# The low part of the attention output in the first four chunks: by a product with minus one and a copy, in place of a subtraction

## The chip, the cores and the metric

The kernel runs on one core of a Trainium2 chip. The time is the device time of one execution in microseconds; several executions are timed and the median is given. Of one more execution there is a profile, with the start and duration of every instruction on every engine. The engines are TensorE (PE in the profile; its weight loads have a row of their own, PEld), VectorE (DVE), ScalarE (ACT), GpSimd (POOL) and SyncE (SP, which here only issues transfers). PSUM is the memory into which TensorE writes, in eight banks of 128 x 512 words; SBUF holds everything else.

## What is computed

A recurrence over time (linear attention with a decay per channel and a bonus `u` for the current step), and behind it a block with a hidden layer, a convolution over three steps in time and a gate:

```python
for t in range(S):                                   # B=4, H=8, S=768, D=48
    kt, vt, rt, wt = (k[:, :, t], v[:, :, t], r[:, :, t], w[:, :, t])
    cur = np.einsum('bhd,bhe->bhde', u[None] * kt, vt)
    y[:, :, t] = np.einsum('bhd,bhde->bhe', rt, state + cur)
    state = wt[:, :, :, None] * state + np.einsum('bhd,bhe->bhde', kt, vt)
x = y.transpose(0, 2, 1, 3).reshape(B, S, 384)
h = np.maximum(x @ w_in, 0)                          # 384 -> 1024
conv_out = sum(conv_w[j] * shifted(h, j - 1) for j in range(3))
out = (h * sigmoid(conv_out)) @ w_out                # 1024 -> 384
```

The inputs are drawn as float32 for `r`, `k`, `v`, `w` and `u`; the three weights of the block come as float64.

## The kernel before, in words

**Chunks.** The recurrence is taken in chunks of 128 time steps, six to each of the four batches, 24 in all. `stage_a` (lines 527 to 605) loads `w`, `k`, `r` of a chunk, turns them with TensorE (L542), forms the running products of the decays with two scans on VectorE (L549, L556; between them L553 writes the reciprocal of a chunk's whole decay into the buffer `dA`, which L556 reads), scales keys and queries (L554, L560), and writes the diagonal of the bonus on GpSimd (L581, L583, L587). `stage_b` (lines 607 to 746) forms the products of keys and queries (L660), masks them on VectorE (L664), carries the state (L636, L639, L677, L681) and makes the output `y` of the chunk, turned, in a bank of PSUM.

**High and low parts.** The block's products take numbers of the type float32r. To keep the accuracy, every factor is split: a high part, which is the number cast to float32r, and a low part, the difference of the number and its high part. A product of two factors is then three products, high by high, high by low and low by high (`product_in`, L753, and `product_out`, L782). The tile `xT` holds the chunk outputs, turned, with high (index 0) and low (index 1) parts beside each other; `wi` and `wo` hold the weights, split in the same way (L456 casts, L457 subtracts), after they have been put together from the words of the float64 (L436 to L450).

**The first four chunks** (`n < EARLY`, with `EARLY = 4`) are made in another layout than the rest, so that the first block needs no transfer from SBUF to SBUF. Their `y` is made in rows of 128 by L690, L693, L700 and L705. ScalarE copies it as the high part into `xT` (L708); VectorE subtracts that from `y` for the low part (L709). The other twenty chunks do the same in L731 and L733.

**Blocks.** Eight blocks of 384 time steps follow their chunks. Each goes through eight slices of the hidden layer: three times three products (L753), relu, convolution and gate on ScalarE and VectorE (L765 to L772), the split (L774, L775); then the products with `wo` (L782), a copy (L812) and the transfer out (L813). The first block needs the chunks 0 to 3, since the convolution reaches one step beyond its 384.

**The order.** Nothing of this is issued as it is written. Each step is put into a plan with `op(engine, cost, function, reads, writes, ...)`, with a cost in microseconds from the table `LEN` and a rank (chunk n: 14 n; its second stage 7 later; a block 5 per slice later still). `Plan.issue` (lines 139 to 221) then runs a list scheduler: each engine takes, of the steps that are ready and for which a buffer is free, the one of lowest rank. Steps of TensorE count 1.4 times their cost in the first 60 us (`COLD`). The order thus found is the fixed order of each engine's queue. Buffers come from kinds with a number of places (`Kind`): eight PSUM banks shared by five kinds, two places for `dA` and so on; a place comes free when the last step that uses it is done. A changed cost, step or number of places can change the order of everything after it.

Ahead of the plan, the constants are made, among them the 128x128 identity `ident` on GpSimd.

Of the kernel before, what the change touches and what calls it, by code (L numbers as in the profile page):

```python
# [9 lines left out]
F32 = mybir.dt.float32  # L10
BF16 = mybir.dt.bfloat16
F32R = mybir.dt.float32r
# [3 lines left out]
ALU = mybir.AluOpType  # L16
# [19 lines left out]
    stt=0.54, gate=0.47, wts=0.47, wstt=0.47,  # L36
    fill=0.25, kh=0.42, guard=0.72, sbd=0.34, xhi=0.49, relu=0.5, mul=0.49, sig=0.43, cast=0.42, out=0.37, exp=0.52,
    z=0.98, diag=1.07, lo=0.97,
    gather=1.6, carried_rows=1.4, y_rows=1.5,
    load=0.55, issue=0.45, spread=0.64,  # L40
)
TAIL = dict(PE=0.22, DVE=0.11, ACT=0.13, POOL=0.07, SP=2.2)
# [66 lines left out]
class Plan:  # L109
# [6 lines left out]
    def op(self, eng, us, f, r=(), w=(), holds=(), moves=0.0, port=False, rank=None):  # L116
        i, deps = len(self.ops), set()
        us = LEN[us] if isinstance(us, str) else us
        for t in r:
            if t in self.last:  # L120
                deps.add(self.last[t])
            self.readers.setdefault(t, []).append(i)
        for t in w:
            if t in self.last:
                deps.add(self.last[t])
            deps.update(self.readers.get(t, ()))
            self.last[t], self.readers[t] = i, []
        deps.discard(i)
        bufs = []
        for t in (*r, *w, *holds):  # L130
            if isinstance(t, Buf) and t not in bufs:
                bufs.append(t)
                t.uses += 1
                if t.turn is None:
                    t.turn = t.kind.wanted
                    t.kind.wanted += 1
        self.ops.append((eng, us, f, deps, bufs, moves, port, (self.rank if rank is None else rank) + i * 1e-6))
# [159 lines left out]
def rwkv_conv_moe_kernel(  # L297
# [12 lines left out]
    nc = tc.nc  # L310
# [3 lines left out]
    P = 128  # L314
# [5 lines left out]
    KT = DM // P  # L320
    WID = KT * SL + 1
# [8 lines left out]
    fconst = fast.enter_context(tc.tile_pool(name="fconst", bufs=1))  # L330
# [8 lines left out]
    for _ in range(WARM):  # L339
# [8 lines left out]
    ident = const.tile([P, P], F32, name="ident")  # L348
# [5 lines left out]
                            fill=0.0, base=0, channel_multiplier=-1)  # L354
# [13 lines left out]
    guard_hi = fconst.tile([P, 1], F32, name="guard_hi")  # L368
    nc.vector.memset(guard_hi, -W_HI)
    flags = fconst.tile([P, N, 2], F32, name="flags")  # L370

    xT = const.tile([P, 2 * KT + 1, 2, SP2], F32R, name="xT")
    nc.gpsimd.memset(xT[:, :, :, 0:1].bitcast(F32), 0.0)
# [7 lines left out]
    def kind(name, n, shape, dtype=F32, fill=None):  # L381
        tiles = [fconst.tile(shape, dtype, name=f"{name}{i}") for i in range(n)]
        for t in tiles:
            if fill:
                fill(t)
        return Kind(n, (tiles, []))
# [3 lines left out]

    nat = {nm: kind(nm, 2, [P, H, 64]) for nm in "wkr"}
    nat["v"] = kind("v", 3, [P, H, D])
    dA_k = kind("dA", 2, [P, WID], fill=lambda t: nc.vector.memset(t, 0.0))

    kr_k = kind("kr", 3, [P, 2, WID], fill=lambda t: nc.gpsimd.memset(t[:, :, 0:WID:WID - 1], 0.0))
    last_k = kind("last", 2, [R, 2, SL + 1], fill=lambda t: nc.gpsimd.memset(t, 0.0))
# [22 lines left out]
    op = plan.op  # L419
# [98 lines left out]
    def pairs(t):  # L518
        return t[0:R].rearrange("p (m t) -> p m t", t=L)

    def thirds(t):
        return t[:, 0:KT * L].rearrange("p (m t) -> p m t", t=L)
# [84 lines left out]
    def stage_b(n):  # L607

        b, c = divmod(n, NCH)
        st = chunks[n]  # L610
        odd = b % 2
        kr, kh, pm, last, vN = (st[x] for x in ("kr", "kh", "pm", "last", "v"))
# [5 lines left out]
        def rt(m):  # L618
            return kr.t[0:R, 1, m * SL:m * SL + L] if m < KT else last.t[:, 1, 0:L]
# [7 lines left out]
        if early:  # L627
            vx = Buf(vx_k)
            op("ACT", "fill", lambda: nc.scalar.copy(
                out=vx.t[:, :, :, D:64], in_=vN.t[:, 2 * KT:H].rearrange("p g (m i) -> p m g i", m=KT)), [vN], [vx])  # L630
        if c:
            sd, sbd = Buf(sd_k), Buf(sbd_k)
            if early:
# [3 lines left out]
                out=sd.t[:, 0:KT], in0=old.t[:, 0:KT], in1=kr.t[0:R, 0, 1:WID:SL].unsqueeze(2).to_broadcast([R, KT, D]),  # L637
                op=ALU.mult), [old, kr], [sd], port=True)
            op("DVE", "small", lambda: nc.vector.tensor_scalar(  # L639
                out=sd.t[:, KT], in0=old.t[:, KT], scalar1=last.t[:, 0, 1:2], scalar2=None, op0=ALU.mult),  # L640
                [old, *lasts], [(sd, 1)], [sd, last], port=True)
            for g in range(2):
                p = slice(64 * g, 64 * g + D)
                if early:
                    op("ACT", "sbd", lambda g=g, p=p: nc.scalar.copy(
                        out=sbd.t[p, 0:KT, 64 * g:64 * g + D], in_=sd.t[p, 0:KT]),
                        [sd], [sbd] if g == 0 else [(sbd, 1)], [sbd])
                    op("ACT", "fill", lambda g=g, p=p: nc.scalar.copy(
                        out=sbx.t[p, :, 64 * g + D:64 * g + 64], in_=sd.t[p, KT].rearrange("p (m i) -> p m i", m=KT)),
# [13 lines left out]
        for g in range(2):  # L663
            op("DVE", "cp", lambda g=g: nc.vector.copy_predicated(  # L664
                out=pm.t[:, g], mask=upper.unsqueeze(1).to_broadcast([P, NP, L]),
                data=sc[g].t.rearrange("p (m t) -> p m t", t=L)), [sc[g], pm], [(pm, g)])
        if c < NCH - 1:
            t = Buf(pb)
# [15 lines left out]
        y = Buf(pb)  # L684
        ts = slice(1 + c * L, 1 + (c + 1) * L)
        if early:
            if c:
                def carried_rows():
                    for m in range(KT):
                        nc.tensor.matmul(y.t[:, m * L:(m + 1) * L], lhsT=sbx.t[:, m, :], rhs=rt(KT),  # L690
                                         start=(m == 0), stop=False, skip_group_check=True)
                    for m in range(KT):
                        nc.tensor.matmul(y.t[0:R, m * L:(m + 1) * L], lhsT=sbd.t[:, m, :], rhs=rt(m),  # L693
                                         start=False, stop=False, skip_group_check=True)
                op("PE", "carried_rows", carried_rows, [sbd, (sbd, 1), sbx, (sbx, 1), kr, (kr, 1), *lasts], [y], [last])

            def within_rows():
                for m in range(KT):
                    for g in range(2):
                        nc.tensor.matmul(y.t[64 * g:64 * g + 64, m * L:(m + 1) * L], lhsT=vx.t[:, m, g, :],  # L700
                                         rhs=pm.t[:, g, KT, :], start=(c == 0 and m == 0), stop=False,
                                         skip_group_check=True)
                for m in range(KT):
                    for g in range(2):
                        nc.tensor.matmul(y.t[64 * g:64 * g + D, m * L:(m + 1) * L], lhsT=vN.t[:, 2 * m + g, :],  # L705
                                         rhs=pm.t[:, g, m, :], start=False, stop=True, skip_group_check=True)
            op("PE", "y_rows", within_rows, [vx, vN, pm, (pm, 0), (pm, 1)], [y])
            op("ACT", "kh", lambda: nc.scalar.copy(out=xT[:, 0:KT, 0, ts], in_=thirds(y.t)), [y], [("x", odd, c, 0)])  # L708
            op("DVE", "kt", lambda: nc.vector.tensor_tensor(  # L709
                out=xT[:, 0:KT, 1, ts], in0=thirds(y.t), in1=xT[:, 0:KT, 0, ts].bitcast(F32), op=ALU.subtract),  # L710
                [y, ("x", odd, c, 0)], [("x", odd, c, 1)])
            return
        if c:
            def carried():
# [5 lines left out]
        def within():  # L720
# [13 lines left out]
            out=xT[0:R, slots, 1, ts], in0=pairs(y.t), in1=xT[0:R, slots, 0, ts].bitcast(F32), op=ALU.subtract),  # L734
# [5 lines left out]
        for g in range(2):  # L740
            for m in range(KT):
                op("SP", "spread", lambda g=g, m=m: nc.sync.dma_start(
                    out=xT[64 * g + D:64 * g + 64, (KT + 1) * odd + m, :, tg].bitcast(F32),
                    in_=xT[64 * g + 16 * m:64 * g + 16 * m + 16, KT, :, tg].bitcast(F32)),
# [107 lines left out]
    for n in range(N + 1):  # L852
        if n < N:
            plan.rank = CHUNK * n - LEAD - AHEAD
            loads(n)
            plan.rank = CHUNK * n - LEAD
            stage_a(n)
            plan.rank = CHUNK * (n + 0.5) - LEAD
            stage_b(n)
        while bi < len(blocks) and blocks[bi][0] * NCH + min((blocks[bi][1] + HB) // L, NCH - 1) <= n:  # L860
            block(*blocks[bi], HB, CHUNK * (3 * bi + 4), bi == len(blocks) - 1)
            bi += 1
# [11 lines left out]
        out=inside, in0=total.t[0:1, 0:1], scalar1=0.0, scalar2=None, op0=ALU.is_le), [total], ["inside"])  # L874
# [35 lines left out]
```

## Time and profile before

| | |
|---|---|
| median of 3 runs | 385.2 us (384.16 to 385.79) |
| the profiled execution | 383.74 us, span 382.0 us, mean granted TensorE clock 0.969 |
| busy in the span | PE 353.0, PEld 322.2, DVE 285.7, ACT 234.9, POOL 174.3 us |
| matmuls | 2794; L753 576 of them (124.5 us), L782 576 (123.3 us) |
| DVE and ACT instructions | 575 and 612 |

In the rows of the profile "line engine operation out<-in" names the group, then come its form (partitions x elements, type) and its count; in brackets stands how long the engine stood idle before and what ended that. Busy times of TensorE overlap, since matmuls are pipelined, and those of VectorE and ScalarE a little too: a queue's price of an instruction is the distance from its start to the next start. Where stretches of the span are listed, each row has the stretch, its length, the busy time and number of instructions of each engine named in the header, then the granted TensorE clock (1.00 is full), the share of the DMA engines and GB/s. A row of waits reads: engine, tile and line that waited, what it waited for, microseconds in total, times, the longest.

### The profile page before, as it was taken

How to read it: one execution, taken by the hardware profiler on the slowest of the kernel's cores; microseconds unless marked ns; L12 is line 12 of the kernel's file. 1: busy time of each engine (PE TensorE's matmuls, PEld its weight loads, DVE VectorE, ACT ScalarE, POOL GpSimd, SP SyncE). 2: the span in 40 equal slices, each digit the busy share in tenths (PEclk: the TensorE clock that was granted, in tenths of full speed). 3: DMA queues.
4: the chain of work that ended last, by engine and by line, in shares of the span. 5: the costliest groups of instructions: out<-in, count | busy, mean ns of one | idle time of the engine just before them, and what ended most of it. 6: DMA issues, size and time to landing. Idle time of an engine off the chain costs nothing.

```text
span 382.0 us, 7869 instructions
## 1 busy us (share of the span) xinstructions
PE 353.0 (92%) x2794; PEld 322.2 (84%) x2794; DVE 285.7 (75%) x575; ACT 234.9 (61%) x612; POOL 174.3 (46%) x199
## 2 busy tenths in 40 slices
PE   6839578898899999999999999999999999999994
PEld 3728557787699999998999989998999998999993
DVE  1668999999987986778787786768879755863640
ACT  5145646898766763498648652696775625765741
POOL 5536758857854343066533450373543410332430
PEclk9977698999999999999999999999999999999998
DMA  8989993524433443543343253824334121010001
GB/s 162 129 151 172 267 241 82 115 50 79 82 75 69 100 102 53 133 98 82 74 92 85 55 106 75 165 51 99 78 85 82 33 51 57 0 44 21 22 22 66
DMA packets 116623, 34.44 MB, mean 90 GB/s; under 512 B 106146, under 2 KB 113827, under 8 KB 116579
## 3 DMA queue, kind: packets, MB, share of 16 engines
q1 hardware_dynamic: 116578, 33.89, 43.0%
q8 instruction: 23, 0.38, 0.4%
q14 instruction: 22, 0.17, 0.2%
HBM read 25.19 MB, written 4.72 MB: 78 GB/s over the span
## 4 chain that ended last, share of the span: by engine, by line
PE 73%; DVE 14%; DMA 3%; issue 3%; SPq 2%; POOL 2%; ACT 1%; DVEq 0%; POOLq 0%
PE bank L782 26%; PE bank L753 24%; PE bank L660 5%; PE bank L542 5%; PE bank L726 5%; PE bank L716 4%; DMA gh<-in_moe_w_in_dram 2%; PE bank L677 2%; PE bank L595 2%; SPq L502 1%; DVE kr L549 1%; DVE kr L556 1%; DVE wide L447 1%; DVE bank L444 1%; DVE bank L436 1%
## 5 line engine op out<-in xcount | busy, mean ns | idle before, releaser
L753 PE MATMUL bank<-xT,wi 128*128 128x386 f32 x576 | 124.5, 346 | 0.0
L782 PE MATMUL bank<-wo,gh 128*128 128x384 f32 x576 | 123.3, 343 | 0.0
L775 POOL TENSOR_TENSOR gh<-g,gh 128x384 fp32r<-128x384 f32 x64 | 64.5, 1013 | 111.3 <-ACT gh L774 105.9
L753 PEld LDWEIGHTS bank<-xT,wi 128*128 128x128 f32 x576 | 100.3, 189 | 2.9 <-issue 2.2
L782 PEld LDWEIGHTS bank<-wo,gh 128*128 128x128 f32 x576 | 99.5, 188 | 1.7 <-issue 0.9
L767 DVE SCALAR_TENSOR_TENSOR a<-bank,cw,a 128x384 f32<-128x384 f32 x64 | 38.2, 609 | 22.6 <-ACT a L766 22.6
L587 POOL TENSOR_SCALAR_AFFINE_SELECT pm<-dg 128x1024 f32<-128x1024 f32 x24 | 26.4, 1099 | 51.0 <-PE bank L726 44.8
L771 ACT ACTIVATE a<-a 128x384 f32<-128x384 f32 x64 | 33.4, 523 | 21.9 <-DVE a L769 21.7
L772 DVE TENSOR_TENSOR g<-bank,a 128x384 f32<-128x384 f32 x64 | 34.6, 547 | 11.3 <-ACT a L771 10.6
L765 ACT ACTIVATE bank<-bank 128x386 f32<-128x386 f32 x64 | 30.4, 476 | 20.3 <-PE bank L753 19.0
L664 DVE COPY_PREDICATED pm<-upper,bank 128x512 f32<-128x512 int32 x48 | 33.3, 726 | 10.5 <-PE bank L660 10.3
L769 DVE SCALAR_TENSOR_TENSOR a<-bank,cw,a 128x384 f32<-128x384 f32 x64 | 38.2, 609 | 0.6
L774 ACT CAST gh<-g 128x384 fp32r<-128x384 f32 x64 | 32.3, 511 | 9.7 <-DVE g L772 9.4
L766 ACT ACTIVATE a<-bank,cw 128x384 f32<-128x384 f32 x64 | 36.2, 579 | 0.4
L549 DVE TENSOR_TENSOR_SCAN kr<-bank,one_end 128x387 f32<-128x387 f32 x24 | 23.0, 957 | 15.9 <-PE bank L542 15.8
L581 POOL TENSOR_TENSOR z<-r,k 128x384 f32<-128x384 f32 x24 | 24.3, 1012 | 14.0 <-DMA r<-in_r_dram 14.0
L583 POOL TENSOR_TENSOR z<-z,ubc 128x384 f32<-128x384 f32 x24 | 24.3, 1011 | 4.3 <-ACT ubc L511 3.2
L660 PEld LDWEIGHTS bank<-kr 48*128 48x128 f32 x288 | 19.9, 202 | 6.7 <-issue 4.6
L660 PE MATMUL bank<-kr 48*128 48x128 f32 x288 | 24.7, 305 | 0.4 <-DVE g L772 0.4
L812 ACT COPY wide<-bank 128x384 f32<-128x384 f32 x24 | 11.5, 480 | 21.9 <-PE bank L782 21.4
L569 PE MATMUL bank<-kr,sel 128*112 128x130 f32 x48 | 10.9, 386 | 14.2 <-DVE kr L554 7.0
L556 DVE TENSOR_TENSOR_SCAN kr<-bank,dA 128x387 f32<-128x387 f32 x24 | 22.8, 952 | 0.0
(106 smaller groups left out, 542.2 us busy)
## 6 DMA issues: line engine op xcount, KB each, us to landing
w<-in_w_dram SPq DMA_DIRECT2D x24, 192.0 KB, 3.4
k<-in_k_dram SPq DMA_DIRECT2D x24, 192.0 KB, 3.5
r<-in_r_dram SPq DMA_DIRECT2D x24, 192.0 KB, 3.8
v<-in_v_dram SPq DMA_DIRECT2D x24, 192.0 KB, 3.5
out_dram<-wide SPq DMA_DIRECT2D x24, 192.0 KB, 2.0
gh<-in_moe_w_out_dram SPq DMA_DIRECT2D x2, 1152.0 KB, 9.2
last<-kr SPq DMA_DIRECT2D x120, 16.2 KB, 1.8
gh<-in_moe_w_in_dram SPq DMA_DIRECT2D x4, 432.0 KB, 7.2
```

Source lines behind the costliest of these rows:

```text
L660: nc.tensor.matmul(sc[g].t[:, m * L:(m + 1) * L], lhsT=kt(m)[p], rhs=rt(m)[p], start=True, stop=True)
L664: op("DVE", "cp", lambda g=g: nc.vector.copy_predicated(out=pm.t[:, g], mask=upper.unsqueeze(1).to_broadcast([P, NP, L]), data=sc[g].t.rea ...
L753: nc.tensor.matmul(t.t[:, 0:HB + 2], lhsT=wi[:, m, a, f * P:(f + 1) * P], rhs=xT[:, x0 + m, c, xs], start=(m == 0 and j == 0), stop=(m == ...
L765: ("ACT", "relu", lambda: nc.scalar.activation(out=h(0, width + 2), in_=h(0, width + 2), func=AF.Relu), [t], [t]),
L766: ("ACT", "mul", lambda: nc.scalar.mul(out=a(), in_=h(1), mul=cw[:, 1, bass.ds(f, 1)]), [t, "cw"], [a1]),
L767: ("DVE", "stt", lambda: nc.vector.scalar_tensor_tensor(out=a(), in0=h(0), scalar=cw[:, 0, bass.ds(f, 1)], in1=a(), op0=ALU.mult, op1=ALU. ...
L769: ("DVE", "stt", lambda: nc.vector.scalar_tensor_tensor(out=a(), in0=h(2), scalar=cw[:, 2, bass.ds(f, 1)], in1=a(), op0=ALU.mult, op1=ALU. ...
L771: ("ACT", "sig", lambda: nc.scalar.activation(out=a(), in_=a(), func=AF.Sigmoid), [], [a1]),
L772: ("DVE", "gate", lambda: nc.vector.tensor_tensor(out=g.t[:, 0:width], in0=h(1), in1=a(), op=ALU.mult), [t, a1], [g]),
L774: ("ACT", "cast", lambda: nc.scalar.copy(out=part(0)[:, 0:width], in_=g.t[:, 0:width]), [g], [key]),
L775: ("POOL", "lo", lambda: nc.gpsimd.tensor_tensor(out=part(1)[:, 0:width], in0=g.t[:, 0:width], in1=part(0)[:, 0:width].bitcast(F32), op=AL ...
L782: nc.tensor.matmul(acc.t[:, 0:DM], lhsT=part(a)[:, tt * P:(tt + 1) * P], rhs=wo[:, f, c, :], start=(f == 0 and a + c == 0), stop=(f == FT ...
```

## The change

In the first four chunks, the subtraction on VectorE is replaced by two steps. TensorE multiplies the high part with minus one times the identity (`less`, a float32r tile made once by ScalarE) and adds this onto `y` in its bank, so that the bank then holds the low part. ScalarE copies the bank into `xT`. The product has the cost `rest` in the plan, 0.3 us, the copy that of the first copy, 0.42. The number of places for `dA` goes from two to one.

```diff
-    gather=1.6, carried_rows=1.4, y_rows=1.5,
+    gather=1.6, rest=0.3, carried_rows=1.4, y_rows=1.5,
...
     flags = fconst.tile([P, N, 2], F32, name="flags")
+    less = fconst.tile([P, P], F32R, name="less")
+    nc.scalar.mul(out=less, in_=ident, mul=-1.0)
...
-    dA_k = kind("dA", 2, [P, WID], fill=lambda t: nc.vector.memset(t, 0.0))
+    dA_k = kind("dA", 1, [P, WID], fill=lambda t: nc.vector.memset(t, 0.0))
...
             op("ACT", "kh", lambda: nc.scalar.copy(out=xT[:, 0:KT, 0, ts], in_=thirds(y.t)), [y], [("x", odd, c, 0)])
-            op("DVE", "kt", lambda: nc.vector.tensor_tensor(
-                out=xT[:, 0:KT, 1, ts], in0=thirds(y.t), in1=xT[:, 0:KT, 0, ts].bitcast(F32), op=ALU.subtract),
-                [y, ("x", odd, c, 0)], [("x", odd, c, 1)])
+            op("PE", "rest", lambda: nc.tensor.matmul(thirds(y.t), lhsT=less, rhs=xT[:, 0:KT, 0, ts], start=False, stop=True,
+                                                      skip_group_check=True), [("x", odd, c, 0)], [y])
+            op("ACT", "kh", lambda: nc.scalar.copy(out=xT[:, 0:KT, 1, ts], in_=thirds(y.t)), [y], [("x", odd, c, 1)])
             return
```

## The prediction

> **What bounds the kernel now.** I read the page first, and of it the slices of the span.
>
> ```profile
> span 382.0 us, 7869 instructions
> PE   6839578898899999999999999999999999999994
> DVE  1668999999987986778787786768879755863640
> PEclk9977698999999999999999999999999999999998
> ```
>
> A slice is 9.55 us. VectorE (DVE) is full from the fifth slice to the eleventh, TensorE (PE) from about the twelfth to the end; the granted clock of TensorE dips in three places, all early. So there are two stages with different limits. The busy times by stage put numbers on them:
>
> ```profile
> core 0: us, PE busy (x) PEld busy (x) DVE busy (x) ACT busy (x) POOL busy (x), PEclk, DMA share, GB/s
> 0.00:34.50 34.50, 24.02 (x157) 18.18 (x158) 19.91 (x48) 14.61 (x44) 18.90 (x43) 0.85 0.99 147
> 34.50:67.00 32.50, 24.04 (x229) 20.73 (x228) 31.80 (x71) 18.91 (x58) 22.16 (x24) 0.84 0.82 199
> 67.00:103.70 36.70, 32.25 (x260) 28.06 (x258) 36.55 (x77) 30.13 (x78) 28.75 (x30) 1.00 0.41 82
> 103.70:376.50 272.80, 272.65 (x2154) 255.19 (x2154) 197.39 (x382) 170.81 (x433) 104.44 (x104) 1.00 0.33 71
> ```
>
> From 103.70 to 376.50 us TensorE is busy for 272.65 of 272.80 us: there the end moves only with TensorE's own work, or with the moment at which this stretch begins. Before it, from 34.50 us on, VectorE is busy for 31.80 + 36.55 = 68.35 of 69.20 us. Its waits, over 34 to 103 us:
>
> ```profile
> DVE bank L436 <- DMA gh<-in_moe_w_in_dram: 0.9, 1, 0.9
> DVE wide L441 <- ACT bank L439: 0.3, 1, 0.3
> ```
>
> That is all: VectorE waits 1.2 us in 69. Ahead of 34.5 us the limit is that transfer of weights. The order of every queue is fixed before the launch, so VectorE's queue between 34.8 and 103 us is a chain without a gap, and the dense stretch of TensorE starts when it lets go.
>
> **Part by part.** The subtraction that goes (L709) and the first copy, which stays and is a measure for the new one (L708):
>
> ```profile
> L709 DVE TENSOR_TENSOR xT<-bank,xT x4: 529/546/558, 25.5 to 67.0; 128x384 fp32r<-128x384 f32 x4
> L708 ACT CAST xT<-bank x4: 474/480/488, 25.0 to 66.1; 128x384 fp32r<-128x384 f32 x4
> ```
>
> An instruction's duration is not its price in a full queue, since the next one starts before it ends. The timeline of VectorE around the four of them:
>
> ```profile
> 25.53 0.56 DVE L709 TENSOR_TENSOR xT<-bank,xT 128x384 fp32r<-128x384 f32 x1 [1.24 <-ACT xT L708]
> ...
> 34.84 0.56 DVE L436 TENSOR_SCALAR bank<-gh 128x384 int32<-128x384 int32 x1 [0.87 <-DMA gh<-in_moe_w_in_dram]
> ...
> 39.83 0.55 DVE L709 TENSOR_TENSOR xT<-bank,xT 128x384 fp32r<-128x384 f32 x1
> 40.29 0.54 DVE L447 SCALAR_TENSOR_TENSOR wide<-gh,bank 128x384 f32<-128x384 uint32 x1
> ...
> 55.29 0.53 DVE L709 TENSOR_TENSOR xT<-bank,xT 128x384 fp32r<-128x384 f32 x1
> 55.74 0.55 DVE L560 TENSOR_TENSOR kr<-bank,kr 128x384 f32<-128x384 f32 x1
> ...
> 65.62 0.95 DVE L556 TENSOR_TENSOR_SCAN kr<-bank,dA 128x387 f32<-128x387 f32 x1
> ...
> 66.99 0.55 DVE L709 TENSOR_TENSOR xT<-bank,xT 128x384 fp32r<-128x384 f32 x1
> 67.46 0.54 DVE L560 TENSOR_TENSOR kr<-bank,kr 128x384 f32<-128x384 f32 x1
> ...
> 69.76 0.16 DVE L553 RECIPROCAL dA<-kr 128x3 f32<-128x3 f32 x1
> ```
>
> *Removed.* From L709's start to the next start it is 40.29 - 39.83 = 0.46, 55.74 - 55.29 = 0.45 and 67.46 - 66.99 = 0.47 us. The first one, at 25.53 us, is ahead of the wait for the weights at 34.84 us, which swallows it: nothing. The other three lie in the full stretch: 0.46 + 0.45 + 0.47 = 1.38 us that VectorE no longer has to work. It is also the most that this edit can take off by itself while the order stays alike.
>
> *Added on TensorE.* Four products of 384 columns with a 128x128 bank. The nearest row is the product into the hidden layer (386 columns, the same kind of number), from the chain of waits and from its line:
>
> ```profile
> 117.95 3.40 PE bank L753 x18
> ...
> L753 PE MATMUL bank<-xT,wi x576: 332/339/447, 67.3 to 364.7; 128*128 128x386 f32 x192
> ...
> 41.89 3.42 PE L569 MATMUL bank<-kr,sel 128*112 128x130 f32 x12 [4.20 <-DVE kr L554]
> 67.29 4.64 PE L753 MATMUL bank<-xT,wi 128*128 128x386 f32 x24
> ```
>
> 3.40 / 18 = 0.19 us of queue, 0.34 us until its result is there. If it ran like the full float products of L569 (3.42 / 12 = 0.285 us for 130 columns at half clock, some 0.42 us for 384 columns at full clock) it would be 0.42. Four are 0.76 to 1.7 us; I take 0.76, because both operands are of L753's kind. All four come before about 68 us, where TensorE stands still for 32.50 - 24.04 = 8.5 us between 34.50 and 67.00 alone and VectorE sets the pace. So I cost them at nothing; if that cover were gone they would cost the 0.76 us.
>
> *Added on ScalarE (ACT).* Four copies of L708's form:
>
> ```profile
> 39.20 0.47 ACT L708 CAST xT<-bank 128x384 fp32r<-128x384 f32 x1
> 39.57 0.27 ACT L629 COPY vx<-v 128x96 f32<-128x96 f32 x1
> ...
> 51.58 0.41 ACT L456 CAST wi<-wide 128x256 fp32r<-128x256 f32 x1 [2.12 <-POOL wide L450]
> ...
> 66.12 0.49 ACT L708 CAST xT<-bank 128x384 fp32r<-128x384 f32 x1 [2.58 <-PE bank L705]
> 66.92 0.44 ACT L597 COPY kh<-bank 128x336 f32<-128x336 f32 x1 [0.30 <-PE bank L595]
> 67.25 0.24 ACT L598 COPY kh<-bank 128x96 f32<-128x96 f32 x1
> 67.38 0.53 ACT L456 CAST wo<-wide 128x384 fp32r<-128x384 f32 x1
> ```
>
> 39.57 - 39.20 = 0.37 us of queue each, 1.5 us in all, on an engine that is busy for 18.91 of 32.50 and 30.13 of 36.70 us: nothing.
>
> *The new path.* The low part now needs high part, product, copy. In chunk 3, after which the first block may begin, the high part is there at 66.12 + 0.49 = 66.61. Product 0.34 and copy 0.48 end at 67.43, without the handing over; the subtraction ended at 66.99 + 0.55 = 67.54, because it stood in VectorE's queue. The path is no longer than before if both new instructions get their turn at once. Two waits are new. TensorE waits for the high part, with the transposes of the next chunk and the first block's products queued behind; ScalarE waits for the product, with L597, L598 and L456 behind. If instead the copy goes behind L597 and L598, it is 67.38 - 66.92 = 0.46 us late, and the 24 products that begin at 67.29 wait for it. I take 0.2 us, between 0 and 0.46, nearer to 0 because the path has 0.1 us in hand.
>
> *One buffer instead of two for dA.* It is written by L553 and read for the last time by L556 of the same chunk. The scan of chunk 3 starts at 65.62, the next chunk's reciprocal at 69.76, on the same in-order engine: the one buffer is free before it is wanted. Nothing, nor can it gain, save one fill ahead of the plan, where VectorE has nothing to hurry for. The making of the minus-one bank, one small ScalarE instruction ahead of the plan, is hidden by the wait for the first inputs.
>
> *Sum.* 1.38 - 0.2 = about 1.2 us earlier. The profiled execution took 383.74 us, 1.74 outside its span of 382.0; I expect some 382.5 of such an execution. The median of the runs, 385.2, is 1.46 above it, and I set the forecast against the median: 385.2 - 1.2 = 384.0 us. Bounds of the parts: 1.38 off at best, and 0.76 + 0.46 = 1.2 on if VectorE's relief should be lost.
>
> *A rule weighed against the trace: the clock.*
>
> ```profile
> 37.70:41.89 4.19, 0.00 (x1) 0.86 1.12 174
> 41.89:47.20 5.31, 5.17 (x24) 0.50 1.06 318
> ...
> 61.20:64.60 3.40, 3.40 (x19) 0.50 0.31 63
> ...
> 54.56 0.92 PE L569 MATMUL bank<-kr,sel 128*112 128x130 f32 x6 [2.00 <-DVE kr L554]
> ```
>
> After TensorE stood still for 4.19 us, it ran at a granted clock of 0.50 for 5.31 us. The new product of chunk 1 falls into that pause, at about 39.20 + 0.47 = 39.7, and cuts it in two of about 2 us. The Trainium skill, "TensorE: Matmul & The Clock Gate" (Part 1), says that the clock is halved after one idle window of about 3.4 us and advises against pauses above some 3 us; by that rule the stretch would keep its full clock. The trace agrees for this pause, but shows a half clock from 61.20 to 64.60 though the longest pause since 47.2 us was the 2.00 us before 54.56, so activity short of full idleness counts too, and one product of 0.2 us may be too little. In my sum it changes nothing either way, since VectorE has no wait there to be saved.
>
> **The rivals.** *The order comes out better.* The planner lays out all the queues again, and every later place may shift. TensorE stands still for 36.70 - 32.25 = 4.45 us between 67.00 and 103.70. If the new order closes half of this beyond what I count, the time is 384.0 - 2.2 = 381.8. For it: less VectorE work in the stage in which it is short. Against it: TensorE's pauses there are waits for VectorE, so most of what can close is in my 1.38 already. 0.27.
>
> *The clock stays up, and it counts.* If the 5.31 us at half clock run at full clock, TensorE is 5.31 / 2 = 2.65 us earlier in its queue; if the new order then has VectorE waiting on it there, the time is 384.0 - 2.65 = 381.4. Against it: VectorE's two waits above are all there are. The rule of the skill named above would bring this about. 0.06.
>
> *The new path stalls the first block, and it gets slower.* ScalarE's queue runs in order, and casts in it wait for GpSimd, at 51.58 us for 2.12 us. If such a cast of `wo` stands ahead of the new copy in chunk 3, the low part comes 2.1 us late, and TensorE stands with the 24 products in hand. VectorE wants their outcome at 72.66:
>
> ```profile
> 70.37 1.01 ACT L765 ACTIVATE bank<-bank 128x386 f32<-128x386 f32 x2 [0.77 <-PE bank L753]
> 72.66 1.13 DVE L767 SCALAR_TENSOR_TENSOR a<-bank,cw,a 128x384 f32<-128x384 f32 x2
> ```
>
> ScalarE takes them up late already (0.77 us of waiting at 70.37), so VectorE would stand for about the same 2.1 us: 2.1 - 1.38 = 0.7 us slower, 385.9. If the pause also halves the clock, the products ahead of 70.37 us take 70.37 - 67.29 = 3.1 us more, 389.0. The middle is 387.4. It is slower from 1.4 us of stall on, and clearly so from 1.4 + 1.9 = 3.3. For it: two engines' queues in place of one. Against it: the planner knows these waits and puts ready work first, and ScalarE waits seldom. 0.17.
>
> *Nothing is gained*, because the shift moves VectorE's relief to where it has slack: 385.2 + 0.7 = 385.9 at worst, with the products paid. 0.10. That the change does not do what it says I see no way for: the products and copies stand in the plan like any other step.
>
> **How the numbers follow.** 0.40 stays for the forecast, 384.0 us; its own range is 383.0 to 385.3, from the bounds of the parts and the spread of the runs (384.16 to 385.79). What a measurement of this kernel can tell from no change is about 0.5%, 1.9 us: faster than 383.3 or slower than 387.1. The forecast case lies mostly within; 0.04 of it I give to its edge below 383.3. Faster is then 0.27 + 0.06 + 0.04 = 0.37. Of the stall 0.13 lies above 387.1, and 0.03 I keep for a worse order without it: slower 0.16. The rest is 0.47. For 8 in 10 the range reaches down to 381.2, past both faster rivals' centres, and up to 387.4, the stall's centre.
>
> **What would show it.** Right: L709 gone; VectorE still without waits between 35 and 102 us with some 1.4 us less busy time before TensorE's dense stretch, which begins at about 102.5 and lasts as long as now; four products of about 0.34 us duration ahead of 68 us and four copies of 0.48. The path: first products of the block at about 67.3 or earlier, no wait above 0.5 us on the new copy. The clock: 0.50 or not after 41.9 us. Wrong: new waits of VectorE in this stretch, a pause of TensorE of 2 us at the first block, or pauses in the dense stretch, which would mean that the order decided and not the work.

## The result, and the profile after

The changed kernel took 382.03 us (median of 15 runs, 380.55 to 384.22), the kernel before 384.72 us beside it (15 runs, 382.69 to 386.25). The ratio is 0.9945 with a 95% interval of 0.9924 to 0.9965: 2.1 us faster, between 1.3 and 2.9. (The two medians lie 2.7 us apart; this document goes by the ratio, which has an interval.) The forecast was 1.2 us. A second measurement (e5 below) gave 0.9919 (0.9892 to 0.9947).

The profiled execution of after took 382.98 us, with a span of 381.2, and that of before 383.74 with 382.0. The two profiles differ by less than the medians do. Executions of one kernel lie over 5 us apart (382.08 to 387.48 us in 29 runs of before beside e5 to e8), so one profile can't carry a difference of 1 us in the whole. Part of this spread arises before VectorE's full stretch: the third of its scans over the decays (L549) starts at 38.51 us in the profile of before, and at 35.73 and 39.37 us in those of two kernels whose queues have the same order (e1 and e10 below). What profiles can show is how the work lies in the queues. The slices of the page of after:

```profile
span 381.2 us, 7866 instructions
PE   6847887897999999999999999999999999999994
DVE  2668999999887886778787676889778845864630
PEclk8778699998999999999999999999999999999999
```

and its stages (the columns are those of the same table of before: PE, PEld, DVE, ACT, POOL, clock, DMA):

```profile
34.50:67.00 32.50, 23.50 (x224) 19.62 (x219) 31.59 (x74) 20.51 (x63) 24.35 (x27) 0.89 0.87 205
67.00:103.70 36.70, 32.61 (x258) 28.86 (x257) 34.74 (x71) 29.41 (x76) 26.98 (x28) 0.95 0.36 73
103.70:376.50 272.80, 271.95 (x2148) 255.20 (x2147) 194.35 (x380) 170.87 (x432) 104.42 (x103) 1.00 0.33 71
```

The dense stretch of TensorE is as full as it was (271.95 of 272.80 us). In the stage before it VectorE is busy for 66.33 us in place of 68.35. The waits of VectorE over 34 to 103 us, the longest ones of TensorE from 60 us on, and last, for comparison, the longest of TensorE from 60 us on in before:

```profile
DVE a L769 <- ACT a L768: 1.4, 1, 1.4
DVE bank L438 <- DMA gh<-in_moe_w_in_dram: 0.8, 2, 0.4
DVE kr L551 <- PE bank L544: 0.5, 1, 0.5
DVE wide L443 <- ACT bank L441: 0.4, 1, 0.4
...
PE bank L597 <- DVE kr L556: 2.7, 2, 2.2
PE bank L755 <- ACT xT L713: 1.5, 1, 1.5
PE bank L718 <- ACT sbd L654: 1.2, 1, 1.2
...
PE bank L677 <- DVE g L772: 1.1, 1, 1.1
```

VectorE now has 3.1 us of waits where it had 1.2. Two of the waits of TensorE are new: 1.5 us at the first block for the new copy (L713), and 2.2 us in one piece for VectorE, where before had none above 1.1. The planner laid out nearly every queue anew, as the timeline of chunk 3 shows, ScalarE first and then TensorE:

```profile
62.10 0.48 ACT L710 CAST xT<-bank 128x384 fp32r<-128x384 f32 x1 [0.69 <-PE bank L707]
64.45 0.56 ACT L441 ACTIVATE bank<-bank,ebias 128x384 int32<-128x384 int32 x1 [1.87 <-DVE bank L438]
64.93 0.44 ACT L599 COPY kh<-bank 128x336 f32<-128x336 f32 x1
65.26 0.49 ACT L713 CAST xT<-bank 128x384 fp32r<-128x384 f32 x1
...
63.08 0.55 PE L597 MATMUL bank<-ident,kr 128*128 128x128 f32 x3 [0.54 <-DVE kr L556]
...
63.71 0.42 PE L711 MATMUL bank<-xT,less 128*128 128x384 f32 x1
63.97 0.34 PE L755 MATMUL bank<-xT,wi 128*128 128x386 f32 x1
65.80 2.39 PE L755 MATMUL bank<-xT,wi 128*128 128x386 f32 x12 [1.49 <-ACT xT L713]
```

The high part is there at 62.10 + 0.48 = 62.58. The product (L711) starts only at 63.71, behind transposes (L597) that wait for VectorE, and the second copy stands behind a step (L441) that waits for VectorE as well. TensorE's first product of the block runs at 63.97, needing only the high part; the second waits until 65.80.

### The profile page after: what moved, and what is told of

Its sections match the earlier page's. It is cut to its first block, busy times and chain, and to the rows that moved or that the text cites. A ratio compares the mean times of both kernels' runs of the same rounds, so it can differ in the third digit from the quotient of the medians.

```text
span 381.2 us, 7866 instructions
## 1 busy us (share of the span) xinstructions
PE 352.1 (92%) x2798; PEld 323.0 (85%) x2798; DVE 279.9 (73%) x570; ACT 236.5 (62%) x617; POOL 174.7 (46%) x199
## 4 chain that ended last, share of the span: by engine, by line
PE 76%; DVE 8%; DMA 7%; ACT 4%; issue 2%; SPq 1%; POOL 1%; DVEq 0%
PE bank L755 27%; PE bank L784 26%; PE bank L662 5%; PE bank L728 5%; PE bank L544 5%; PE bank L718 4%; DMA w<-in_w_dram 4%; PE bank L679 2%; DMA gh<-in_moe_w_in_dram 2%; PE bank L597 2%; DVE wide L449 1%; SPq L504 1%; DVE kr L551 1%; DVE wide L443 1%; DMA wide<-in_u_dram 1%
## 5 line engine op out<-in xcount | busy, mean ns | idle before, releaser
L755 PE MATMUL bank<-xT,wi 128*128 128x386 f32 x576 | 128.3, 350 | 1.5 <-ACT xT L713 1.5
L784 PE MATMUL bank<-wo,gh 128*128 128x384 f32 x576 | 124.7, 344 | 0.2 <-POOL gh L777 0.2
L755 PEld LDWEIGHTS bank<-xT,wi 128*128 128x128 f32 x576 | 101.8, 191 | 4.4 <-issue 2.0
L784 PEld LDWEIGHTS bank<-wo,gh 128*128 128x128 f32 x576 | 100.8, 188 | 2.3 <-issue 1.3
L662 PEld LDWEIGHTS bank<-kr 48*128 48x128 f32 x288 | 18.5, 192 | 5.7 <-issue 4.2
L662 PE MATMUL bank<-kr 48*128 48x128 f32 x288 | 23.2, 295 | 0.0
L728 PE MATMUL bank<-pm,v 128*48 128x128 f32 x320 | 21.6, 277 | 0.0
```

What stands on the lines that cost most here:

```text
L662: nc.tensor.matmul(sc[g].t[:, m * L:(m + 1) * L], lhsT=kt(m)[p], rhs=rt(m)[p], start=True, stop=True)
L728: nc.tensor.matmul(y.t[rows, cs], lhsT=vf[:, h * D:h * D + rows.stop - rows.start], rhs=pm.t[:, g, m, :], start=(c == 0 and m == 0), stop= ...
L755: nc.tensor.matmul(t.t[:, 0:HB + 2], lhsT=wi[:, m, a, f * P:(f + 1) * P], rhs=xT[:, x0 + m, c, xs], start=(m == 0 and j == 0), stop=(m == ...
L784: nc.tensor.matmul(acc.t[:, 0:DM], lhsT=part(a)[:, tt * P:(tt + 1) * P], rhs=wo[:, f, c, :], start=(f == 0 and a + c == 0), stop=(f == FT ...
```

## The experiments

The theories, after the result: *work*, VectorE's relief of three slots (1.38 us) in a full queue gave the time; *order*, the queues that the planner laid out anew gave it, whatever the work; *clock*, the products kept TensorE's clock up. Each ratio is to before, measured beside it; the medians of before were 384.02 us (e1 to e4), 384.78 (e5 to e8) and 383.38 (e9 to e12).

**e1 and e2: work and order, each by itself.** Since the plan is a list of steps with functions, a step can be planned as one thing and issued as another. e1 plans the subtraction and issues the product and copy; e2 plans product and copy and issues the subtraction.

```diff
 e1, in before:
-op("DVE", "kt", lambda: nc.vector.tensor_tensor(... op=ALU.subtract), ...)
+def low():
+    nc.tensor.matmul(thirds(y.t), lhsT=less, rhs=xT[:, 0:KT, 0, ts], start=False, stop=True, ...)
+    nc.scalar.copy(out=xT[:, 0:KT, 1, ts], in_=thirds(y.t))
+op("DVE", "kt", low, ...)
 e2, in after:
-op("PE", "rest", lambda: nc.tensor.matmul(thirds(y.t), lhsT=less, ...), ...)
-op("ACT", "kh", lambda: nc.scalar.copy(out=xT[:, 0:KT, 1, ts], in_=thirds(y.t)), ...)
+op("PE", "rest", lambda: None, ...)
+op("ACT", "kh", lambda: nc.vector.tensor_tensor(... op=ALU.subtract), ...)
```

> The work of the change in the order of before: the plan is made with the subtraction as before, and at its place the product and the copy are issued instead, so that every other instruction keeps its place in its queue. Theory 'work' (VectorE is relieved of three slots of 0.46 us, 1.38 us, in a stretch without waits): 1.0 to 1.4 us faster than before. Theory 'order' (the time came from the queues that the planner laid out anew): within 0.5 us of before, or slower if the two new instructions stand badly in the old queues. Theory 'clock' (the products keep TensorE's clock up in its pauses): a granted clock near 1 after the pauses before 28 us and 41.9 us, and 1 us or more faster.

> The reverse: the order of after, with the subtraction on VectorE issued where the second copy stands, and no product. Theory 'work': the gain is gone, within 0.5 us of before. Theory 'order': most of the 2.1 us stays, 1.5 us or more faster than before.

Measured: e1 383.7 us, ratio 1.0019 (0.9988 to 1.0051). e2 384.35 us, ratio 1.0011 (0.9984 to 1.0039). Neither alone is faster. Against e1, *work* expected at least 1 us and got none; against e2, *order* expected 1.5 us and got none. Both together gave 2.1.

**e3 and e4: VectorE's relief and its opposite, in the order of before.**

```diff
 e3, in before:
+nc.vector.memset(xT[:, 0:KT, 1, 1:1 + EARLY * L].bitcast(F32), 0.0)
...
-op("DVE", "kt", lambda: nc.vector.tensor_tensor(... op=ALU.subtract), ...)
+op("DVE", "kt", lambda: None, ...)
 e4, in before:
-op("DVE", "kt", lambda: nc.vector.tensor_tensor(... op=ALU.subtract), ...)
+op("DVE", "kt", lambda: [nc.vector.tensor_tensor(... op=ALU.subtract) for _ in range(2)], ...)
```

> The order of before, with the subtraction left out and nothing in its place; the low part of the first four chunks is zero and is not computed, so a part of the result is left out. VectorE's relief without any price. Theory 'work': 1.4 us faster than before. Theory 'order': within 0.5 us of before.

> The order of before, with each of the four subtractions issued twice. Theory 'work': three more slots of 0.46 us in the full stretch, 1.4 us slower than before. Theory 'order': within 0.5 us of before.

Measured: e3 384.36 us, ratio 0.9994 (0.9967 to 1.0021); e4 387.15 us, ratio 1.0078 (1.0049 to 1.0107). The memset of e3 stands ahead of the plan, where VectorE then waits 4.9 us for TensorE, and delays nothing. The relief without any price gave 0.2 us in the old order, with 1.38 us (0.9964) just outside the interval; the same work added cost 3.0 us (1.9 to 4.1), about twice its slots. So VectorE does set the pace when work is added to it, and in the old order a relief of the same size was not seen in the time. The profiles of before and of e3 show one place where the relief went. The third, the eighth and the ninth of the scans of VectorE (L549, in e3 L550), first in before, then in e3 with the row of its clock after 101.30 us:

```profile
38.51 0.95 DVE L549 TENSOR_TENSOR_SCAN kr<-bank,one_end 128x387 f32<-128x387 f32 x1
...
101.47 0.95 DVE L549 TENSOR_TENSOR_SCAN kr<-bank,one_end 128x387 f32<-128x387 f32 x1
...
111.67 0.96 DVE L549 TENSOR_TENSOR_SCAN kr<-bank,one_end 128x387 f32<-128x387 f32 x1 [0.80 <-PE bank L542]
```

```profile
37.97 0.95 DVE L550 TENSOR_TENSOR_SCAN kr<-bank,one_end 128x387 f32<-128x387 f32 x1
...
99.75 0.95 DVE L550 TENSOR_TENSOR_SCAN kr<-bank,one_end 128x387 f32<-128x387 f32 x1
...
111.22 0.96 DVE L550 TENSOR_TENSOR_SCAN kr<-bank,one_end 128x387 f32<-128x387 f32 x1 [0.79 <-PE bank L543]
...
101.30:104.70 3.40, 3.40 (x25) 0.52 0.59 118
```

From the third to the eighth scan e3 needs 61.78 us, before 62.96: 1.2 us of the relief are there. From the eighth to the ninth e3 needs 11.47 us, before 10.20: they are gone again. (The ninth waits for TensorE in both.) In e3 TensorE's clock fell to 0.52 for the 3.40 us after 101.30, which are 1.6 us of work lost where TensorE has begun to set the pace; in before it was 1.00 over the same microseconds. That is one execution each. The other profiles in this order fit: e1's and e4's have no half clock there and take 10.21 us each from the eighth to the ninth scan; e9's and e10's (below) have it from 102.5 us on and take 11.57 and 11.36. And the profiled execution of e1, which kept its clock, was the fastest of e1's twelve, 381.21 us against a median of 383.7; but it was also 2.8 us ahead of before at the third scan already. So this is one way in which the relief is lost; whether it is lost so in most executions is not shown.

**e5 to e8: after again, and other orders for the same work.** e6 and e7 do the work of before, planned with a cost of 0.1 and 0.6 us for the four subtractions; e8 does the work of after, planned with 0.2 us for the product.

```diff
 e6, e7, in before:
-op("DVE", "kt", lambda: nc.vector.tensor_tensor(... op=ALU.subtract), ...)
+op("DVE", 0.1, ...)      # e7: 0.6
 e8, in after:
-rest=0.3
+rest=0.2
```

> The changed kernel again, beside before and the three others on one chip. If the gain is real: ratio to before 0.9945, within 0.993 to 0.996, and a second profile of the same order that shows which marks move from run to run. If it was the chip or the moment: within 0.3% of before.

> The work of before, every instruction of it, but planned with a cost of 0.1 us in place of 0.47 for the four subtractions: an order of its own, which differs from that of before about as much as that of after does. Theory 'work': within 0.3% of before. Theory 'order' (each new layout of the queues moves the time by up to 0.5%, whatever the work is): off by 0.3 to 1% either way.

> As the one before, with a planned cost of 0.6 us: a third order for the work of before. Theory 'work': within 0.3% of before. Theory 'order': off by 0.3 to 1% either way.

> The work of after, planned with a cost of 0.2 us in place of 0.3 for the product with minus one: another order for the new work. Theory 'work': 0.3 to 0.5% faster than before, like after. Theory 'order': anywhere within 1% of before, so that after's gain need not come back. Theory 'work and order together' (new work pays only in queues laid out for it): 0.4 to 0.7% faster.

Measured: e5 381.97 us, 0.9919 (0.9892 to 0.9947); e6 384.45 us, 0.999 (0.9961 to 1.002); e7 383.64 us, 0.9983 (0.9957 to 1.0009); e8 383.64 us, 0.9972 (0.9948 to 0.9996). The gain is real. With e2, the old work has now been run in four orders, and the three others than its own move it by -0.17% to +0.11% (intervals from -0.43% to +0.39%): none of these orders is worth the gain by itself, after's own among them, and *order* in its plain form is out. The new work in the two orders planned for it is faster each time (0.9945 and 0.9919 for after, 0.9972 for e8), by sizes that differ; e8's interval all but reaches 1.

**e9 and e10: the clock.** Idle products go into TensorE's pauses, in before and in e1.

```diff
 e9, in before (e10 puts the same tile and products into e1, where dA has one place already):
+    warm = fconst.tile([P, HB], BF16, name="warm")
+    nc.vector.memset(warm, 0.0)
...
-    dA_k = kind("dA", 2, ...)
+    dA_k = kind("dA", 1, ...)
...
 def gather():
+    for _ in range({1: 24, 2: 16, 3: 8}.get(n, 0)):
+        nc.tensor.matmul(gt.t[:, 0:HB], lhsT=warm[:, 0:P], rhs=warm, start=True, stop=True)
```

> Before in its own order, with 24, 16 and 8 idle products of 384 columns put into TensorE's pauses ahead of the gathering products of chunks 1, 2 and 3 (into the bank that these then overwrite), so that the clock stays up; the unused second buffer of dA makes room for their operand. VectorE's work is unchanged. Theory 'work': within 0.3% of before, whatever the clock does. Theory 'clock' (half-clock stretches ahead of 70 us cost time and after has fewer of them): mean granted clock up from 0.964 to about 0.98 and 1 to 2 us faster.

> The same idle products in the kernel that does the new work in the order of before, which gained nothing by itself (ratio 1.0019). If the half clock was what swallowed VectorE's relief there: 0.3 to 0.6% faster than before, and faster than the kernel with the idle products alone. If the old queues swallow it by waits of their own: within 0.3% of before.

Measured: e9 384.89 us, ratio 1.0022 (0.9993 to 1.0051); e10 383.94 us, 1.0011 (0.998 to 1.0043). In e9's profile the pauses of chunks 1 and 2 are filled and the clock is full there, where in before it was low for long after both. The rows of before come first, then those of e9:

```profile
22.00:30.00 8.00, 2.06 (x10) 0.61 0.95 154
38.00:46.00 8.00, 3.97 (x17) 0.67 1.10 234
```

```profile
20.84 4.06 PE L570 MATMUL bank<-warm 128*128 128x384 bf16 x24
38.04 2.76 PE L570 MATMUL bank<-warm 128*128 128x384 bf16 x16 [1.81 <-DVE wide L443]
...
22.00:30.00 8.00, 6.19 (x51) 1.00 1.01 162
38.00:46.00 8.00, 6.96 (x66) 1.00 1.08 289
54.50:61.50 7.00, 6.98 (x52) 0.53 0.18 40
75.00:79.00 4.00, 4.00 (x27) 0.57 0.02 4
102.50:106.50 4.00, 3.97 (x29) 0.57 0.27 56
```

The profiled execution's mean clock was 0.981 (before 0.969), and the kernel was no faster. But the last three rows show half clock at places where before had 0.98, 1.00 and 1.00, the last of them where TensorE begins to set the pace. So e9 shows that filling the early pauses brings no gain, and not what the early half clock costs by itself. *Clock*, as stated, is out for another reason: after's own profile has the half clock behind the same two pauses (rows further down), so its products did not keep the clock up. e10 did not bring back the relief that e1 lost, but it doesn't settle why: in its profile the clock was still 0.62 over 22 to 30 us and 0.79 over 38 to 46, and 0.59 over 102.50 to 106.50. That the half clock near 103 us takes the relief in the old order, and spares it in the new one, is a rival that no run tested by itself.

**e11 and e12: the price of the new path, in the order of after.** e11 issues neither product nor second copy, and sets the low part to zero by the memset of e3. e12 issues both right behind the first copy.

```diff
 e12, in after:
+def both():
+    nc.scalar.copy(out=xT[:, 0:KT, 0, ts], in_=thirds(y.t))
+    nc.tensor.matmul(thirds(y.t), lhsT=less, rhs=xT[:, 0:KT, 0, ts], ...)
+    nc.scalar.copy(out=xT[:, 0:KT, 1, ts], in_=thirds(y.t))
+op("ACT", "kh", both, ...)
+op("PE", "rest", lambda: None, ...)
+op("ACT", "kh", lambda: None, ...)
```

> The order of after, with neither product nor second copy; the low part of the first four chunks is zero and is not computed, so a part of the result is left out. Against after this shows the price of the product and the copy in the new queues. If they are hidden: 0.55 to 0.8% faster than before, like after. If the stall of 1.5 us of TensorE at the first block (seen in after's profile) is paid: 0.9% or more faster than before.

> After, with the product and the second copy issued right behind the first copy in their queues, all else in after's order. The product of chunk 3 no longer stands behind two transposes and the copy no longer behind a step that waits for VectorE. If the stall of 1.5 us at the first block is paid: 0.2 to 0.4% faster than after, 0.9 to 1.1% faster than before. If VectorE sets the pace there anyway: like after.

Measured: e11 382.15 us, ratio 0.9967 (0.9938 to 0.9996); e12 382.29 us, 0.9973 (0.9942 to 1.0005). In e12's profile the stall is gone, the block's first 18 products run in one piece:

```profile
62.52 0.44 PE L712 MATMUL bank<-xT,less 128*128 128x384 f32 x1
62.97 0.55 PE L597 MATMUL bank<-ident,kr 128*128 128x128 f32 x3
63.35 0.49 PE L544 MATMUL bank<-ident,w 128*128 128x128 f32 x3
63.60 3.44 PE L758 MATMUL bank<-xT,wi 128*128 128x386 f32 x18
```

and yet it is not faster than after, nor is e11, which has no new path at all. Both came out at about half of what was expected of a kernel like after, and e12's interval reaches just beyond 1. Product, copy and a stall of 1.5 us at the first block cost nothing that these runs can tell; VectorE has no wait there in after's profile. The three kernels e11, e12 and after all have after's order and no subtraction on VectorE; e2 has the same order with the subtraction and is the one that gains nothing. In this order, then, it is the subtraction that makes the difference: from 0.9945 or 0.9919 (after), 0.9967 and 0.9973 to 1.0011. Those of after are clear of e2's interval; those of e11 and e12 touch it. The ratios lie 0.4% to 0.9% below e2's, 1.5 to 3.5 us against slots of 1.38 us, each known to about 1.5 us (an estimate from the intervals). That the change pays in one order and not in the other is clear for the change as a whole (e1 against after). For the relief without its price, e3's 0.9994 against e11's 0.9967, the intervals overlap.

No version was clearly faster than after.

## Why the prediction held, and where its steps did not

**The bound.** Two stages, VectorE to about 103 us and then TensorE without a gap: the shares of busy time held in every profile (VectorE 65.6 to 68.9 of the 69.2 us, TensorE almost without a gap from about 104 us on). What did not hold is the link between the two: in e3 VectorE was 1.7 us ahead of before at its eighth scan, and 0.45 us at its ninth, which waits for TensorE.

**The size.** 1.2 us were forecast and 2.1 (1.3 to 2.9) came, just beyond my line of 0.5% for a change that a measurement can tell. As a time, 382.03 us is inside the range of 8 in 10, but below the 383.0 to 385.3 that I gave the forecast itself, and next to the 381.8 of the rival of a better order; before took 0.5 us less beside it (384.72) than the 385.2 that I set out from. The term at fault is the 1.38 us for three slots of VectorE, "the most that this edit can take off by itself while the order stays alike". While the order stays alike it took off nothing that could be measured (e1, and e3 with 0.2 us): a queue without gaps for VectorE does not mean that the end follows it when it gets shorter. In the order planned for the new work, removing the same subtraction was worth about its slots or more (e2 against after, e11 and e12). So the work paid only together with an order planned for it, which neither my sum nor any of my rivals said. That the sum came out as near as it did was in part luck.

**The signs.** One sign that I had named as wrong came, new waits of VectorE in its full stretch (3.1 us for 1.2); and the wait for the new copy, 1.5 us, was beyond the 0.5 us of the right case, though short of the 2 us of the wrong one. I had said that such signs would mean that the order decided and not the work. By e2 the order alone gives nothing, so the signs could not tell the two apart.

**The order as a rival.** I priced a better order at 2.2 us on top and gave it 0.27. None of the three orders tried is better by itself (e2, e6, e7). But the new order does hold something that I had not counted: the two steps that scale the state (L636 and L639, in after L638 and L641). Their busy time between 34.5 and 103.7 us, in before and then in after, with the ranges of the second:

```profile
34.50:103.70 69.20, 2.16 (x4) 0.93 0.60 137
34.50:103.70 69.20, 3.21 (x4) 0.93 0.60 137
L639 DVE TENSOR_SCALAR sd<-s,last x20: 222/416/1000, 31.5 to 325.7; 112x48 f32<-112x48 f32 x20
```

```profile
34.50:103.70 69.20, 2.92 (x4) 0.93 0.60 135
34.50:103.70 69.20, 0.96 (x4) 0.93 0.60 135
L641 DVE TENSOR_SCALAR sd<-s,last x20: 234/240/999, 29.9 to 324.5; 112x48 f32<-112x48 f32 x20
```

2.16 + 3.21 = 5.37 us became 2.92 + 0.96 = 3.88, 1.5 us less for the same eight instructions. The figures follow the order and not the work: 2.17 + 3.42 in e1, 2.91 + 0.96 in e2. Against them stands the new wait of VectorE for ScalarE, 1.4 us in after and 1.7 in e2. That the two about cancel would fit e2's ratio, but is not shown: in e11's profile, which has no half clock between 45 and 375 us, this wait is 0.2 us.

**Product and copies at nothing:** held, as far as e11 can tell; the product itself took 0.42 us at full clock, where I had 0.34. **The new path at 0.2 us:** the size was wrong, the stall was 1.49 us in after's profile, and it costs nothing that e12 can tell. My own rival had the mechanism, both queues standing in line behind steps that wait, with a point of 1.4 us from which it should decide; the stall reached that point and decided nothing, and VectorE had other work until the products were due. **One buffer for dA:** with one buffer the planner finds the same order for the old work (e1 and e9 have one); it was timed only together with other edits. The scan at 65.62 us that I called chunk 3's is the fifth of its line, chunk 4's; the argument holds for it all the same, since the next reciprocal is that of 69.76. **The clock:** nothing speaks against my reading that the half clock after the pause changes nothing in the sum, but e9 could not test it cleanly. That the product would keep the clock up was wrong, as my doubt had it; the rows of after:

```profile
24.50:31.50 7.00, 6.26 (x35) 0.51 1.11 184
38.20:45.00 6.80, 5.85 (x24) 0.50 0.99 177
92.60:96.00 3.40, 3.40 (x13) 0.52 0.10 24
```

In after, TensorE waited 3.15 us for the high part of chunk 1 before its product at 38.66, and the clock was at 0.50 from 38.2 on. The rule of the Trainium skill, "TensorE: Matmul & The Clock Gate" (Part 1), names one idle window of about 3.4 us; here a pause a little shorter was enough, and the measurement decides.

**What stays open:** why the old order does not hand on VectorE's relief. The half-clock stretch of e3 at 101.30 us accounts for it in that one execution. The profiles of after, e2, e5 and e12 have such a stretch between 90 and 96.5 us instead and e11's has none, so the new order may owe its gain in part to where the half clock falls. Whether it does so on the mean would take many profiles of one kernel, and was not tried.

## What to carry to other kernels

In this kernel a queue without waits told that work added there is paid for (e4); it did not tell that work taken away is gained (e3). Where a scheduler lays out the queues, hold the order fixed and swap the work, and hold the work and swap the order: only the two together tell what an edit is worth. When an experiment fills one pause, look through the rest of the profile for the same loss at another place (e9). And know how far executions of one kernel lie apart (here 5 us) before a difference between two profiles is read as an effect.

## What the runs showed of the hardware that I had not expected

The same VectorE instruction on 112x48 elements took between 222 and 1000 ns (L639 above), by a pattern that belongs to the order of the queues: nearly the same sums came back in each kernel with that order (four of them took 3.1 to 3.4 us in five of the six profiles in the order of before, 2.4 in e10's, and 0.96 to 0.97 in all those in the order of after). At 46.79 us in before it ends, after 0.81 us, just behind GpSimd's subtraction of 46.56 to 47.56 us:

```profile
46.56 1.00 POOL L457 TENSOR_TENSOR wi<-wide,wi 128x384 fp32r<-128x384 f32 x1 [0.62 <-ACT wi L456]
...
46.79 0.81 DVE L639 TENSOR_SCALAR sd<-s,last 112x48 f32<-112x48 f32 x1
```

All four of L639 in the full stretch of before (0.73 to 0.86 us) end so, 0.04 to 0.05 us behind a GpSimd instruction that was running when they began; the four of after (0.23 to 0.25 us) began while GpSimd was idle. This agrees with the Trainium skill, "SBUF — State Buffer" (its terms, under the shared port pair), by which VectorE and GpSimd share a pair of ports that one of them holds for its whole instruction while the other waits; no run here took GpSimd's work away to show it.

The stretches at half clock in these profiles last 3.4 us, 6.8 us or, in before from 23.8 us on, 10.2 us; one of them, at 92.60 us in after, followed a pause of TensorE of only 2.15 us.
